# Opening of an attention and expert kernel: one more product in three float32r terms, one batch written out, another order

## The chip, the cores and the metric

The kernel runs on one core of one Trainium2 chip. The metric is the device time of one execution in microseconds (us). The kernel before takes 484.51 us, the median of three executions (484.27 to 484.58).

The core has TensorE (PE, matrix products into PSUM), VectorE (DVE), ScalarE (ACT), GpSimd (POOL, idle here), SyncE (SP, which only issues transfers here) and DMA engines that move data between HBM and SBUF.

## The reference

Inputs: `x` (8 batches, 8 heads, 512 rows, 64 columns) and `state` (8, 8, 32, 64) in float32, four weights `w1`, `w2` (512 x 1024), `w3` (1024 x 1024) and `w_out` (1024 x 512), which arrive as float64.

```python
scores = scale * x @ state.T;  a = softmax(scores);   xread = a @ state
scores2 = scale * state @ x.T; a2 = softmax(scores2); sread = a2 @ x
tokens = concat([xread, sread], axis=2)   # 544 rows a batch, 512 columns
out = ((tokens @ w1) * (tokens @ w2)) @ w3 @ w_out
```

## The kernel before, in words

The products `w3 @ w_out` are formed once (called B here, 1024 x 512), so that each batch needs only `g = (tokens w1) * (tokens w2)` and `g B`. Since `xread = a @ state`, `tokens w1` is formed as `a (state w1)`: a small product of states and weights per batch (steps `u`, line 206) and a large one with the attention weights `a` (steps `a0` to `a7`, line 440). From batch 1 on, `g B` is done in quarters with seven products (steps `P1` to `P7`); batch 0 uses plain products (steps `e` and `z`, line 584). The rows of `sread` of all batches are multiplied at the end (line 870).

**Two kinds of matrix product.** A product on float32 operands is one instruction of the program, which the trace shows as two records. For float32r operands a value is split into a high part (a cast on ScalarE, step names that end in `h`) and a low part (a subtraction on VectorE, names that end in `l`), and the product is three instructions: high by low, high by high, low by high.

**The opening.** Every weight arrives as 64-bit words and is turned into float32 in steps of one row block of 128 rows and 1024 columns (`conversion_steps`, line 674): `l` loads 1 MB (SP), `p` reads the high words (ScalarE), `u` the low words (ScalarE, a few on VectorE), `s` shifts (VectorE), `a` and `b` add (VectorE). Blocks `c0` to `c7` hold a row block of `w_out` and half of a column block of `w3`; `w4` to `w7` hold the other halves of `w3`; `q0` to `q7` hold `w1` and `w2`. B is the sum over k of products of row block k of `w3` (transposed) and row block k of `w_out`: step `f{k}` (line 749, matmuls in line 763) adds the term k for the first four row blocks of B, step `m{i}{k}` (line 786, matmuls in line 798) the term k for row block i from 4 to 7. For the k in `THIN` (line 39) `f{k}` uses three float32r terms; its operands are split by the steps `v{k}oh`, `v{k}ol` (rows of `w_out`) and `v{k}wh`, `v{k}wl` (columns of `w3`). For the k in `THIN_W3` (line 40) `m{i}{k}` does so, with the steps `V{i}h`, `V{i}l`. The steps `k...` split B.

**Attention steps of batch b.** `x` loads states and x (lines 270, 272), `sP` multiplies them (line 206), `sM` to `sl` are the two softmaxes, `sQ` a rearrangement by 16 transfers, `rP` the product for `sread`, `t` the load of x in another layout.

**What sets the order.** The order is written out by hand: `OPENING` (line 42) is a list of step names, of which `follow` (line 912) calls one after the other, and each engine gets its instructions in that order. `OPENING` covers the weights and batch 0, with pieces of batch 1. For the batches 1 to 7 `follow` runs a script (`SCRIPTS`, line 61), in which `+` stands for a step of the next batch; `CLOSING` ends the kernel. Each engine works its own list in order and waits only where a step needs the result of another engine. Transfers are all issued in one list by SP; a load into a buffer waits until the steps that read what was there before are done, and the loads behind it in the list wait with it. x of a batch is loaded into the buffer `x_d`, which in the opening first holds the words of `c4` (`HOMES`, line 36); the words of `c3` and `w4` lie in the buffer `x_s`.

Of the kernel before, what the change touches and what calls it, by code (L numbers as in the profile page):

```python
# [33 lines left out]
WARM = 15  # L34
CUTS = {"c0": (320, 640, NW), "c1": (640, NW)}
HOMES = {"c3": "x_s", "c4": "x_d", "w4": "x_s", "q0": "x_s"}
LOADS = {}
ON_DVE = ("c0u0", "c0u1", "c1u0", "c2u0")
THIN = (2, 4, 6)
THIN_W3 = {4: (2, 4, 6), 5: (2, 4, 6), 6: (2, 4, 6), 7: (2, 4, 6)}  # L40

OPENING = """
c0l c0u0 c0p0 c1l c0p1 c0p2 c0u2 c0s0 c0u1 c0s1 c1p1 c0s2 c0a0 c0b1 c0a1 c0b2 c1p0 c1u0 c1u1 c1s1 c2l c1s0 f0
c3l c4l c1b1 c2p0 c1a0 c1b0 c2u0 c5l c2s0 c2a0 f1 c2b0 v2oh v2wh c3p0 c3u0 v2ol v2wl c3s0 c4p0 c3b0 c3a0 c4s0 f2
c6l c4u0 c5p0 c4a0 v4oh f3 c7l c4b0 v4wh c5u0 v4ol v4wl c5s0 c5a0 w4l c5b0 c6p0 c6u0 w5l c6s0 c7p0 f4 c6a0 v6oh
c6b0 v6wh c7s0 c7u0 v6ol w4p0 w6l w4u0 v6wl c7b0 w5p0 w4s0 f5 c7a0 f6 w5u0 f7 w6p0 0:x 0:sP w4a0 w5s0 w5a0 V4h
w6s0 q1l V4l k0h k0l q0l w7l V5h m40 V5l 0:sT m42 k1h m47 m44 m45 q1p0 k1l m46 w6u0 0:sR q0p0 m50 q1s0 q1u0 m52
w6a0 m41 m43 w7p0 m51 w7u0 V6h k4h m55 0:sM m56 q0s0 kph q1a0 w7s0 m53 0:sN 0:sS m57 w7a0 k4l 0:sX q2l 0:sC kpl
q0u0 m54 q2p0 q3l 0:sD m60 m61 q0a0 k5h k5l q3p0 0:sF m67 V7h m63 q4l q2u0 V7l 0:sE m70 m73 m65 0:sG m77 q5l
q2s0 q3s0 V6l m71 0:sV q3u0 m75 m72 q3a0 m74 m64 0:sh q2a0 q4p0 q4u0 q6l 0:q00p 0:q01p 0:sl 0:q11p 0:q00h 0:q01h  # L50
0:q11h 0:sW q5p0 m62 0:q00l 1:x 0:q01l q4s0 m66 0:q11l q4a0 q5u0 k6h 0:q10p q5s0 m76 0:q10h q6u0 q6p0 k7h 0:a0
0:q10l q7l 0:sQ k6l q5a0 0:c0 q6s0 q7u0 0:m0 k7l 0:h0 q6a0 0:l0 0:a1 0:a2 0:c1 0:e0 q7p0 q7s0 0:m1 0:c2 0:u2p
q7a0 0:m2 0:u3p 0:a3 0:h1 0:u2h 0:u3h 0:h2 0:u2l 0:u3l 0:c3 0:l1 0:sA close 0:a5 0:a4 0:l2 g00 0:m3 0:h3 g01
0:l3 0:c5 g0A g0C 0:sB g0B 0:c4 0:m5 0:m4 1:sP 0:e1 g0D 0:e2 0:h4 0:a6 0:a7 0:h5 1:sT 0:l5 1:sR g11 1:sS 0:e3
0:l4 1:sM g10 1:sX 0:c6 0:t 0:c7 1:sC 0:m6 g0h 0:m7 2:x 1:sD 0:h7 0:e4 0:h6 1:sN g0l 0:l6 0:e5 0:e6 g1A 1:sE
0:l7 1:sF 0:e7 g1B 1:sA 0:rP g1D 1:u0p g1C 1:sB g1h 1:sG 0:rS 0:o0 1:u1p g1l 1:u2p g20 0:z3 1:sV 0:rV g21 1:u0h
1:sh g2A 0:o1 g2C 1:sl g2B 1:t 1:u0l 0:d0 g2D 1:sW 0:z2 g30 g2h g2l g3A 1:sQ g31 g3C g3B 0:d1 0:o3 1:u1h 0:o2
g3D 1:u2h 0:d3 0:rQ 1:u1l 1:u2l g3h g3l 0:d2
"""

SCRIPTS = {
# [48 lines left out]
def attn_bilinear_kernel(  # L110
# [11 lines left out]
    B, _, NT, H, D = x_s.shape  # L122
# [35 lines left out]
    def step(name):  # L158
        def keep(f):
            assert name not in steps, name  # L160
            steps[name] = f
            return f

        return keep
# [509 lines left out]
    def conversion_steps(name, src, place, wout=None):  # L674
# [7 lines left out]
        def _():  # L682
            c["out"] = place() if callable(place) else place
            room, tag, bufs = (att, HOMES[name], 1) if name in HOMES else (pool, "raw", 3)
            c["raw"] = room.tile([P, NW], mybir.dt.int64, name=tag, bufs=bufs)
            loads = LOADS.get(name, ())
            for start, stop in zip((0, *loads), (*loads, NW)):
# [39 lines left out]
    for k in range(FT):  # L727
        conversion_steps(f"c{k}", w34_k[k], chunks[k], w_out[k])

        if k in THIN:  # L730
            @step(f"v{k}oh")
# [18 lines left out]
        def _(k=k):  # L750
# [4 lines left out]
            for i in range(FT // 2):  # L755
                cols = slice(i * P, (i + 1) * P)
                if k in THIN:
                    hi, lo = thin[k, 0]
# [153 lines left out]
    def follow(script, b=None):  # L912
        for name in script.split():
            ahead = {"+": 1, "*": 2}.get(name[0], 0)
            if b is None or name[0] == "!":
                key = name.lstrip("!")
            elif b + ahead < B:
                key = f"{b + ahead}:{name.lstrip('+*')}"
            else:
                continue  # L920
            steps[key]()

    follow(OPENING)
    for b in range(1, B):
        follow(SCRIPTS.get(b, SCRIPTS[None]), b)
    follow(CLOSING)

# [43 lines left out]
```

## Time and profile before

| | us |
|---|---|
| median of three executions | 484.51 |
| the profiled execution | 484.38 |
| its span, from the first to the last instruction | 482.6 |
| TensorE: matmuls in flight | 476.6 |
| VectorE busy | 394.4 |
| ScalarE busy | 238.7 |

The rows of the trace are told apart by engine, source line and operation, with output and input tile; times are us from the start of the span. `PEld` is the load of weights into the array, which lies beside the matmuls. A matmul's record begins when it is let into the array and ends at a modelled time, so records overlap and the distance from start to start is the time that a matmul really takes of the engine. TensorE ran at the full clock (mean 0.999) through the profiled execution.

### The profile page before, as it was taken

The page shows a single profiled execution, that of the slowest core. Times are in us where ns is not written, and L with a number is a line of the kernel's source. Part 1 is how long each engine was busy: PE and PEld are TensorE (multiplying, and loading weights), DVE is VectorE, ACT ScalarE, POOL GpSimd, SP SyncE. Part 2 cuts the span into 40 slices and gives each one's busy share as a digit, 9 for nine tenths or more (in the row PEclk, how much of TensorE's full clock was granted, in tenths as well). Part 3 has the DMA queues.
Part 4 walks back from the last instruction along what each step waited for, and adds up shares of the span by engine and source line. Part 5 has one row for each costly group of instructions (what it writes and reads, how often), then busy time and mean ns, then how long its engine had stood idle before and what let it go on. Part 6 is the DMA issues. An engine that isn't in the chain of part 4 may idle for free.

```text
span 482.6 us, 8676 instructions
## 1 busy us (share of the span) xinstructions
PE 476.6 (99%) x3414; PEld 375.1 (78%) x3414; DVE 394.4 (82%) x589; ACT 238.7 (49%) x376; POOL 0.2 (0%) x4
## 2 busy tenths in 40 slices
PE   8999999999999999999999999999999999999996
PEld 6545476867779777978797879787978797899885
DVE  5899997997998599859985998599859985578870
ACT  4989784534555055505551554156425632353640
POOL 0000000000000000000000000000000000000000
PEclk9999999999999999999999999999999999999999
DMA  8999653234015304230523042304220222001001
GB/s 342 428 422 372 264 140 96 87 111 107 11 53 176 89 4 182 48 87 4 182 46 88 4 183 48 84 5 183 50 84 4 90 53 80 6 2 64 26 1 44
DMA packets 56361, 52.49 MB, mean 109 GB/s; under 512 B 42752, under 2 KB 50944, under 8 KB 51712
## 3 DMA queue, kind: packets, MB, share of 16 engines
q1 hardware_dynamic: 47488, 43.27, 26.7%
q10 hardware_dynamic: 8832, 8.65, 5.2%
q8 instruction: 27, 0.44, 0.4%
q14 instruction: 14, 0.11, 0.1%
HBM read 38.27 MB, written 8.91 MB: 98 GB/s over the span
## 4 chain that ended last, share of the span: by engine, by line
PE 97%; DMA 1%; ACT 0%; DVE 0%; issue 0%
PE ps L440 37%; PE ps_o L226 11%; PE ps L237 8%; PE ps L206 8%; PE ps_o L584 7%; PE ps_o L231 6%; PE ps_o L798 5%; PE ps L242 4%; PE ps L870 3%; PE ps_o L763 3%; PE ps L763 3%; PE ps L872 2%; PE ps_o L385 1%; DMA raw<-in_w_k_dram 1%; ACT w_sb L696 0%; PE ps L385 0%
## 5 line engine op out<-in xcount | busy, mean ns | idle before, releaser
L440 PE MATMUL ps<-at_lo,sw_hi 128*128 128x512 f32 x256 | 100.6, 393 | 0.0
L440 PE MATMUL ps<-at_hi,sw_lo 128*128 128x512 f32 x256 | 99.9, 390 | 0.0
L440 PE MATMUL ps<-at_hi,sw_hi 128*128 128x512 f32 x256 | 99.9, 390 | 0.0
L450 ACT COPY tmp<-ps 128x512 f32<-128x512 f32 x64 | 37.5, 586 | 125.0 <-PE ps L440 122.6
L440 PEld LDWEIGHTS ps<-at_lo,sw_hi 128*128 128x128 f32 x256 | 48.1, 188 | 11.1 <-issue 0.8
L440 PEld LDWEIGHTS ps<-at_hi,sw_lo 128*128 128x128 f32 x256 | 48.1, 188 | 10.1
L440 PEld LDWEIGHTS ps<-at_hi,sw_hi 128*128 128x128 f32 x256 | 48.1, 188 | 9.7
L182 DVE TENSOR_TENSOR tmp<-tmp,ps 128x512 f32<-128x512 f32 x50 | 34.3, 686 | 18.8 <-PE ps L242 17.0
L179 DVE TENSOR_TENSOR sw_lo<-ps,sw_hi 128x1024 fp32r<-128x1024 f32 (+1 forms) x34 | 38.4, 1149 | 5.4 <-ACT sw_hi L185 5.4
L465 DVE TENSOR_TENSOR g_x<-tmp,ps 128x512 f32<-128x512 f32 x28 | 19.0, 677 | 28.0 <-ACT tmp L450 28.0
L185 ACT CAST g_hi<-raw 128x512 fp32r<-128x512 f32 x42 | 24.7, 619 | 31.3 <-DVE raw L465 21.9
L185 ACT CAST sw_hi<-ps 128x1024 fp32r<-128x1024 f32 (+1 forms) x34 | 31.3, 971 | 4.5 <-PE ps L206 4.5
L226 PEld LDWEIGHTS ps_o<-t,g_hi 128*128 128x128 f32 x224 | 27.7, 190 | 5.0 <-PE ps L206 5.0
L206 PE MATMUL ps<-w_sb,st 64*32 64x512 f32 (+1 forms) x544 | 31.4, 570 | 0.0
L185 ACT CAST g_hi<-g_x 128x512 fp32r<-128x512 f32 x42 | 25.5, 626 | 11.2 <-DVE g_x L465 6.0
L179 DVE TENSOR_TENSOR g_lo<-raw,g_hi 128x512 fp32r<-128x512 f32 x42 | 27.4, 679 | 3.6 <-ACT g_hi L185 2.0
L226 PE MATMUL ps_o<-t,g_hi 128*128 128x256 f32 x224 | 29.6, 285 | 0.0
L226 PE MATMUL ps_o<-wo,g_hi 128*128 128x256 f32 x224 | 29.0, 282 | 0.0
L226 PEld LDWEIGHTS ps_o<-wo,g_hi 128*128 128x128 f32 x224 | 28.2, 189 | 0.5
L237 PE MATMUL ps<-t,g_hi 128*128 128x512 f32 x112 | 28.0, 392 | 0.0
L179 DVE TENSOR_TENSOR g_lo<-g_x,g_hi 128x512 fp32r<-128x512 f32 x42 | 27.1, 682 | 1.0 <-PE ps_o L231 1.0
L237 PEld LDWEIGHTS ps<-t,g_hi 128*128 128x128 f32 x112 | 20.2, 189 | 3.6
(139 smaller groups left out, 813.0 us busy)
## 6 DMA issues: line engine op xcount, KB each, us to landing
x_d<-in_x_d_dram SPq DMA_DIRECT2D x8, 1024.0 KB, 8.1
x_s<-in_x_s_dram SPq DMA_DIRECT2D x8, 1024.0 KB, 5.2
raw<-in_w_dram SPq DMA_DIRECT2D x7, 1024.0 KB, 7.0
out_dram<-tmp ACTq DMA_DIRECT2D x56, 128.0 KB, 1.8
raw<-in_w_k_dram SPq DMA_DIRECT2D x6, 1024.0 KB, 9.6
e<-work SPq DMA_DIRECT2D x112, 32.0 KB, 2.0
raw<-in_w3t_dram SPq DMA_DIRECT2D x3, 1024.0 KB, 6.3
sread<-turned SPq DMA_DIRECT2D x128, 4.0 KB, 1.7
```

The costliest lines, as they stand in the source:

```text
L179: nc.vector.tensor_tensor(out=out, in0=x, in1=y, op=ALU.subtract)
L182: nc.vector.tensor_tensor(out=out, in0=x, in1=y, op=ALU.add)
L185: nc.scalar.copy(out=hi, in_=src)
L206: nc.tensor.matmul(ps[j * NS:(j + 1) * NS, q], states[rows, j], moving(rows, j), start=True, stop=True)
L226: nc.tensor.matmul(ps[:, tt * HO:(tt + 1) * HO], g, w(part, k), start=(fresh and k == 0 and tt == 0 and part == "lo"), stop=False, skip_gr ...
L231: nc.tensor.matmul(ps[:, tt * HO:(tt + 1) * HO], g, w("hi", k), start=False, stop=(k == QF - 1), skip_group_check=True)
L237: nc.tensor.matmul(ps[:, tt].rearrange("p (n d) -> p n d", n=2), g, w(k), start=(k == 0), stop=False, skip_group_check=True,)
L440: nc.tensor.matmul(ps[:, i], w[:, kt, c:c + P], a[:, kt], start=(k == 0), stop=(k == 3 * KT - 1))
L450: nc.scalar.copy(out=copies[ft], in_=sums[ft][:, 0])
L584: nc.tensor.matmul(ps[:, :DO], g, wo[w][:, ft, :], start=(ft == 0 and k == 0), stop=(ft == FT - 1 and k == 2))
L763: nc.tensor.matmul(w34_ps[i][:, :DO], a, w, start=(k == 0 and n == 0), stop=(k == FT - 1 and n == len(terms) - 1))
L798: nc.tensor.matmul(w34_ps[i][:, :DO], a, w, start=(len(started) == 1 and n == 0), stop=(len(started) == FT and n == len(terms) - 1),)
```

## The change

Three things change. Row 7 joins `THIN`, so f7 is done in three float32r terms, and the steps v7oh, v7ol, v7wh and v7wl come in. Batch 1 leaves the loop: the loop starts at `LOOPED = 2`, and all steps of batch 1 (and those of batches 2 and 3 that its script held) are written into `OPENING`. The order in `OPENING` is another one throughout. `THIN_W3` is as before, so the steps m47, m57, m67 and m77 stay in float32.

```diff
+LOOPED = 2
 ON_DVE = ("c0u0", "c0u1", "c1u0", "c2u0")
-THIN = (2, 4, 6)
+THIN = (2, 4, 6, 7)
 THIN_W3 = {4: (2, 4, 6), 5: (2, 4, 6), 6: (2, 4, 6), 7: (2, 4, 6)}
 
 OPENING = """
-c0l c0u0 c0p0 c1l c0p1 c0p2 c0u2 c0s0 c0u1 c0s1 c1p1 c0s2 c0a0 c0b1 c0a1 c0b2 c1p0 c1u0 c1u1 c1s1 c2l c1s0 f0
...
+c0l c0p0 c0u0 c1l c0p1 c0u1 c0s1 c0s0 c0a1 c0a0 c0p2 c0u2 c0s2 c0b1 c1p0 c2l c3l c0b2 c1u0 c1p1 c1u1 c1s0 c1s1
...
     follow(OPENING)
-    for b in range(1, B):
+    for b in range(LOOPED, B):
         follow(SCRIPTS.get(b, SCRIPTS[None]), b)
     follow(CLOSING)
```

The line numbers of the changed kernel are higher by 7 (line 763 is 770, line 798 is 805).

VectorE at the very start, before: c0 is converted in pieces of 320, 320 and 384 columns; 128x320 rows with `ulps` are the low words (c0u0, c0u1), those on `w_sb` the shifts (c0s0, c0s1; 384 columns: c0s2), and `ISA` rows the sums, whose sizes count half words (640: c0a0, 256: c0b1, 384: c0a1, 768: c0b2).

```order
L707 TENSOR_SCALAR ulps<-raw 128x320
L714 TENSOR_SCALAR w_sb<-w_sb 128x320
L707 TENSOR_SCALAR ulps<-raw 128x320
L714 TENSOR_SCALAR w_sb<-w_sb 128x320
L714 TENSOR_SCALAR w_sb<-w_sb 128x384
L721 ISA w_sb<-w_sb,ulps 128x640
L721 ISA w_sb<-w_sb,ulps 128x256
L721 ISA w_sb<-w_sb,ulps 128x384
L721 ISA w_sb<-w_sb,ulps 128x768
```

The same place now:

```order
L714 TENSOR_SCALAR ulps<-raw 128x320
L714 TENSOR_SCALAR ulps<-raw 128x320
L721 TENSOR_SCALAR w_sb<-w_sb 128x320
L721 TENSOR_SCALAR w_sb<-w_sb 128x320
L728 ISA w_sb<-w_sb,ulps 128x384
L728 ISA w_sb<-w_sb,ulps 128x640
L721 TENSOR_SCALAR w_sb<-w_sb 128x384
L728 ISA w_sb<-w_sb,ulps 128x256
L728 ISA w_sb<-w_sb,ulps 128x768
```

The low words come first, and the short shift c0s2 has moved from before the three sums that f0 needs to before the last of them.

TensorE at the end of the f products, before: rows with `w_sb` alone on the right are float32 (f7 at the first two), those with `g_hi,tmp` and `g_lo,tmp` float32r (the row ahead is the last of f6), `x_d,st` is 0:sP, and line 798 is m40 and m42.

```order
L763 MATMUL ps_123<-g_hi,tmp 128x512
L763 MATMUL ps_o<-w_sb 128x512 x2
L763 MATMUL ps_123<-w_sb 128x512 x2
L206 MATMUL ps_277<-x_d,st 32x512 x8
L798 MATMUL ps_o<-w_sb,w_202 128x512
L798 MATMUL ps_o<-g_hi,g_x 128x512
```

Now, from f5 to the beginning of f6:

```order
L770 MATMUL ps_o<-w_sb 128x512 x2
L770 MATMUL ps_128<-w_sb 128x512 x2
L213 MATMUL ps_239<-x_d,st 32x512 x8
L770 MATMUL ps_o<-g_hi,tmp 128x512
L770 MATMUL ps_o<-g_lo,tmp 128x512
L770 MATMUL ps_o<-g_hi,tmp 128x512 x2
```

The product 0:sP has moved from behind f7 to between f5 and f6, and f7, which follows f6, is made of the same rows as f6.

SP's list of loads, before: `raw`, `x_s` and `x_d` are the buffers, `w_k` the blocks c, `w3t` the blocks w, `w` alone the blocks q, `in_st` and `in_x_d` are step 0:x.

```order
L688 DMA raw<-in_w_k_dram 128x1024 x3
L688 DMA x_s<-in_w3t_dram 128x1024
L688 DMA raw<-in_w3t_dram 128x1024 x2
L270 DMA st<-in_st_dram 128x128
L272 DMA x_d<-in_x_d_dram 128x2048
L688 DMA raw<-in_w_dram 128x1024
```

Now:

```order
L695 DMA raw<-in_w_k_dram 128x1024 x3
L277 DMA st<-in_st_dram 128x128
L279 DMA x_d<-in_x_d_dram 128x2048
L695 DMA x_s<-in_w3t_dram 128x1024
L695 DMA raw<-in_w3t_dram 128x1024 x2
L695 DMA raw<-in_w_dram 128x1024
```

The states and x of batch 0 have moved ahead of w4, w5 and w6 in the list.

## Rows read from the trace of the kernel before

**Rows 1.** The page's first part: busy us of each engine, share of the span, instructions.

```profile
PE 476.6 (99%) x3414; PEld 375.1 (78%) x3414; DVE 394.4 (82%) x589; ACT 238.7 (49%) x376; POOL 0.2 (0%) x4
```

**Rows 2.** Busy time of each engine in three stretches: start and end, length, then per engine busy us (instructions), the granted clock of TensorE, the busy share of the DMA engines, GB/s.

```profile
8.33:34.15 25.82, 25.72 (x77) 14.25 (x78) 23.80 (x39) 23.46 (x29) 0.00 (x0) 1.00 1.01 426
34.15:63.40 29.25, 29.25 (x157) 15.66 (x158) 28.30 (x36) 23.88 (x31) 0.00 (x0) 1.00 0.84 330
63.40:139.80 76.40, 76.40 (x546) 57.69 (x546) 68.63 (x107) 38.54 (x60) 0.00 (x0) 1.00 0.27 73
```

**Rows 3.** The chain of work that ended last, in order of time: start, length, engine, tile and line.

```profile
8.33 1.98 PE ps_o L763 x4
...
27.84 1.38 PE ps_o L763 x6
...
30.61 1.72 PE ps_o L763 x4
32.33 1.72 PE ps L763 x4
34.15 1.09 PE ps L206 x16
35.24 23.61 PE ps_o L798 x67
...
63.40 8.17 PE ps L440 x36
...
170.94 16.55 PE ps L440 x72
...
478.70 0.58 ACT tmp L906
```

**Rows 4.** What TensorE's matmuls waited for in the whole execution: us in total, times, longest.

```profile
PE ps_o L149 <- DVE work L146: 1.0, 1, 1.0
PE ps_o L763 <- DVE w_sb L721: 0.9, 1, 0.9
```

**Rows 5.** The end of f7 and 0:sP in order of time (start, length, engine; in brackets the idle time before), and the instruction that loads x of batch 0 (duration in ns, first and last start in us) with its time from issue to landing.

```profile
32.17 1.88 PE L763 MATMUL ps<-w_sb 128*128 128x512 f32 x4
34.15 1.09 PE L206 MATMUL ps<-x_d,st 64*32 64x512 f32 x16
...
34.12 0.21 PEld L206 LDWEIGHTS ps<-x_d,st 64*32 64x32 f32 x16 [0.90 <-issue]
...
L272 SPq DMA_DIRECT2D x_d<-in_x_d_dram x1: 423/423/423, 24.7 to 24.7; - x1
...
DMA to landing us min/median/max: 9.3/9.3/9.3
```

**Rows 6.** The issues of the loads of c4 (`x_d`) and w4 (`x_s`) in order of time, and from the page's sixth part their KB and us from issue to landing.

```profile
2.83 0.45 SPq L688 DMA_DIRECT2D x_d<-in_w_k_dram  x1
...
16.57 0.33 SPq L688 DMA_DIRECT2D x_s<-in_w3t_dram  x1
...
x_d<-in_w_k_dram SPq DMA_DIRECT2D x1, 1024.0 KB, 12.7
x_s<-in_w3t_dram SPq DMA_DIRECT2D x1, 1024.0 KB, 8.7
```

**Rows 7.** ScalarE in order of time: the starts of c0, c1 and c2 (in brackets the idle time before, and what ended it), the low words of c4, a cast of v6 and the low words of c7, then the two steps of w4.

```profile
5.69 1.32 ACT L696 ACTIVATE w_sb<-raw 128x320 f32<-128x320 f32 x3 [3.69 <-DMA raw<-in_w_k_dram]
...
8.10 1.25 ACT L696 ACTIVATE w_sb<-raw 128x384 f32<-128x384 f32 x2 [0.63 <-DMA raw<-in_w_k_dram]
...
10.54 1.18 ACT L696 ACTIVATE w_sb<-raw 128x1024 f32<-128x1024 f32 x1 [0.74 <-DMA raw<-in_w_k_dram]
...
17.43 1.19 ACT L709 ACTIVATE ulps<-x_d 128x1024 int32<-128x1024 uint32 x1
...
25.60 0.62 ACT L185 CAST tmp<-w_sb 128x512 fp32r<-128x512 f32 x1
26.13 1.16 ACT L709 ACTIVATE ulps<-raw 128x1024 int32<-128x1024 uint32 x1
27.17 1.14 ACT L696 ACTIVATE w<-x_s 128x1024 f32<-128x1024 f32 x1
28.21 1.16 ACT L709 ACTIVATE ulps<-x_s 128x1024 int32<-128x1024 uint32 x1
```

**Rows 8.** VectorE in order of time: the start of c0, the sum that completes w4, two long and two short instructions of the stretch after it.

```profile
6.70 0.71 DVE L714 TENSOR_SCALAR w_sb<-w_sb 128x320 int32<-128x320 int32 x2
7.32 1.43 DVE L721 CUSTOM_DVE_ANT_0 w_sb<-w_sb,ulps 128x640 uint16<-128x640 uint16 x4
...
29.56 1.22 DVE L721 CUSTOM_DVE_ANT_0 w<-w,ulps 128x2048 uint16<-128x2048 uint16 x1
...
43.47 1.22 DVE L179 TENSOR_TENSOR work<-work,m 128x1024 f32<-128x1024 f32 x1
44.61 1.22 DVE L721 CUSTOM_DVE_ANT_0 sw_lo<-sw_lo,ulps 128x2048 uint16<-128x2048 uint16 x1
45.74 0.68 DVE L179 TENSOR_TENSOR wo<-ps_o,wo 128x512 fp32r<-128x512 f32 x1
46.35 1.22 DVE L336 TENSOR_REDUCE sum<-work 128x32 f32<-128x1024 f32 x1
```

**Rows 9.** ScalarE's longest wait for a load between 25 and 62 us: us in total, times, longest.

```profile
ACT w_sb L696 <- DMA raw<-in_w_dram: 2.2, 1, 2.2
```

More of the change, by code (lines that the diff above doesn't have):

```diff
@@ L36 @@
 HOMES = {"c3": "x_s", "c4": "x_d", "w4": "x_s", "q0": "x_s"}
+LOOPED = 2
 LOADS = {}
 ON_DVE = ("c0u0", "c0u1", "c1u0", "c2u0")
-THIN = (2, 4, 6)
+THIN = (2, 4, 6, 7)
 THIN_W3 = {4: (2, 4, 6), 5: (2, 4, 6), 6: (2, 4, 6), 7: (2, 4, 6)}
 OPENING = """
-c0l c0u0 c0p0 c1l c0p1 c0p2 c0u2 c0s0 c0u1 c0s1 c1p1 c0s2 c0a0 c0b1 c0a1 c0b2 c1p0 c1u0 c1u1 c1s1 c2l c1s0 f0
-c3l c4l c1b1 c2p0 c1a0 c1b0 c2u0 c5l c2s0 c2a0 f1 c2b0 v2oh v2wh c3p0 c3u0 v2ol v2wl c3s0 c4p0 c3b0 c3a0 c4s0 f2
-c6l c4u0 c5p0 c4a0 v4oh f3 c7l c4b0 v4wh c5u0 v4ol v4wl c5s0 c5a0 w4l c5b0 c6p0 c6u0 w5l c6s0 c7p0 f4 c6a0 v6oh
@@ L46 @@
[L46 to L55, printed above, removed]
@@ L56 @@
-0:l7 1:sF 0:e7 g1B 1:sA 0:rP g1D 1:u0p g1C 1:sB g1h 1:sG 0:rS 0:o0 1:u1p g1l 1:u2p g20 0:z3 1:sV 0:rV g21 1:u0h
-1:sh g2A 0:o1 g2C 1:sl g2B 1:t 1:u0l 0:d0 g2D 1:sW 0:z2 g30 g2h g2l g3A 1:sQ g31 g3C g3B 0:d1 0:o3 1:u1h 0:o2
-g3D 1:u2h 0:d3 0:rQ 1:u1l 1:u2l g3h g3l 0:d2
+c0l c0p0 c0u0 c1l c0p1 c0u1 c0s1 c0s0 c0a1 c0a0 c0p2 c0u2 c0s2 c0b1 c1p0 c2l c3l c0b2 c1u0 c1p1 c1u1 c1s0 c1s1
+c1b0 c1a0 c1b1 f0 c2p0 c4l c5l c2u0 c2s0 c2b0 c2a0 v2wh v2oh c3p0 v2wl v2ol c3s0 c3u0 c6l c3b0 c4p0 c3a0 c4u0
+c4s0 c4b0 f1 c7l c5p0 c4a0 v4wh v4wl f2 v4oh v4ol c5s0 c5u0 c6p0 f3 0:x c6u0 c5a0 c5b0 f4 c6s0 c7p0 c6a0 c7u0
@@ new lines @@
+c6b0 c7s0 v6wh f5 w4l 0:sP w5l v6oh c7a0 c7b0 v7oh w4p0 v7wh w6l v6ol v6wl w4u0 w5p0 v7ol f6 w4s0 v7wl 0:sT f7
+k0h q1l q0l w4a0 k0l 0:sR w5s0 w5u0 V4h w6p0 m40 V4l k1h m45 0:sS w7l m43 w5a0 m44 q1p0 m47 m42 k1l 0:sM 0:sX
+m50 w6s0 q1s0 q1u0 m46 w6u0 m41 V5h m55 w7p0 0:sC k4h m57 V5l q1a0 m52 q0p0 w7u0 w6a0 m51 k4l q2l m54 m56 V6h
+m53 0:sD m60 q0s0 q2p0 m63 kph 0:q01p m67 k5h 0:sF V6l 1:x 0:sN w7s0 0:sG w7a0 m66 k5l 0:sE q3l m70 0:sV q0u0
+q0a0 q5l q2s0 q3p0 m71 m77 q2u0 m73 m65 V7h q3u0 V7l m74 m76 kpl q3s0 m61 q2a0 0:q01h 0:sh q3a0 q5p0 m64 0:q00p
@@ new lines @@
+0:q01l 0:q11p q5u0 q7l 0:q10p 0:q00h 0:sl 0:q11h m62 q4l q7p0 0:q00l q7u0 m75 k6h 0:a0 q5s0 m72 0:q10h q6l
+0:q11l q4p0 0:a1 q5a0 0:c0 k6l q7s0 0:q10l 0:a2 0:m0 q7a0 q4s0 q6p0 0:h0 k7h 0:l0 q6u0 q4u0 q6s0 0:c1 0:c2 k7l
+q6a0 0:e0 q4a0 0:m1 0:m2 0:u3p 0:sW 0:h1 0:u3h 0:u2p 0:u2h 0:u3l close 0:a3 0:u2l 0:l1 0:sA 0:c3 g01 0:a4 0:a5
+0:m3 0:h3 0:l3 0:c4 0:m4 0:h2 0:l2 g00 g0A 0:a7 0:h4 g0B 0:c5 0:sQ g0C 0:m5 0:t 1:sP 0:l4 g0D 0:c7 1:sT 0:a6
+0:m7 0:h7 g10 0:e1 0:e2 1:sM 0:c6 g0h 1:sR 0:m6 0:h5 1:sN 0:h6 0:e3 0:l5 0:sB 0:e4 0:e5 0:l6 0:e6 0:l7 1:sE 1:sS
@@ new lines @@
+1:sX g0l 1:sC 0:e7 g11 0:rP g21 1:t g1A 0:rS 1:sD g1B g1C 1:u1p 0:o0 g1D 1:sF 1:u1h 0:o1 1:u0p 1:sG 0:d1 1:sV
+g1h g20 1:u0h 1:sA g1l 1:u2p 0:z2 g2A g2C 1:sW 2:x 1:u2h 1:sh 0:rV g2B 1:sB g2D 1:u0l 1:u1l 1:sl 0:z3 0:d0 0:o3
+0:d3 1:a0 1:a1 1:u2l 1:c0 0:o2 1:sQ 1:m0 1:u3p g2h 1:c1 1:u3h 2:sP 1:rP g30 g2l 0:d2 1:m1 g31 1:u3l 2:sM 1:a2
+1:c2 2:sN 2:sT g3A g3B 2:sR 2:sS 1:a3 2:sE 1:m2 1:c3 1:a4 0:rQ g3C 2:sX 1:m3 1:A0h g3D 1:rS g3h 1:B1d 2:sC 1:a6
+g3l 1:A1h 1:a5 1:B1h 2:sD 1:A0l 2:sF 1:c6 2:sA 3:x 1:c4 1:c5 1:m4 1:B1l 1:m6 1:a7 1:B0d 2:sG 2:sV 1:A1l 1:B0h
@@ L59 @@
+1:m5 1:c7 1:m7 1:rV 1:B0l 2:sW 1:C0h 1:D0x 1:P1 1:P2 1:E0h 2:u0p 1:E0l 1:D1x 2:u2p 1:v2 1:C1h 2:sQ 2:u1p 1:C0l
+1:v1 1:C1l 2:u0h 1:D0y 1:P3 1:D1y 1:E1h 1:E1l 1:P4 1:G0h 1:rQ 2:u0l 2:u2h 1:F0h 1:F1h 1:v3 1:F1l 1:D0z 1:H0h
+2:u2l 1:G1h 2:t 1:G1l 2:u1h 1:F0l 1:d3 1:P5 2:u1l 1:D1z 1:v5a 1:G0l 1:H0l 1:H1h 2:sh 1:v5b 1:H1l 1:v5c 2:sl 1:P6
+1:v6a 1:v6b 2:sB 1:v6c 1:P7 1:v7a 1:v7b 1:d5 1:d6 1:d7
 """
```

## Prediction

> **What bounds the kernel now.** I read the summary of the engines first [rows 1]: TensorE has a matmul in flight for 99% of the span, VectorE 82%, ScalarE 49%. A share of busy time alone would not settle it, so I went to TensorE's waits: the whole execution has two, of 1.0 and 0.9 us, both before the first real matmul at 8.33 us [rows 4]. Then the chain of work that ended last [rows 3]: from 8.33 us it is TensorE alone, piece against piece, until the closing copy at 478.70 us, and its pieces run at their own pace: 72 float32r matmuls of 512 columns in 16.55 us are 230 ns each, in the middle of the loop as well as in the opening. The table of stretches [rows 2] says the same for the part that is rewritten: TensorE is busy for all but 0.1 us of 8.33 to 139.80 us, while VectorE has 28.3 of 29.25 us between 34.15 and 63.40 us and is nearly full too.
>
> So a new order can win time in three ways only: less work on TensorE, an earlier first matmul, or the closing of the one small hole that a busy share hides. All else that moves on VectorE and ScalarE is worth nothing while TensorE has its operands in time, and costs as soon as it has not.
>
> **The hole.** The step 0:sP (line 206, states against x of batch 0) starts at 34.15 us. The four records before it begin at 32.17 [rows 5]; such records stand 430 ns apart (four in 1.72) [rows 3], so the array was free at 33.89: 0.26 us unused. The weight load of 0:sP came at 34.12 after 0.90 us, and the transfer of x, issued at 24.70, landed 9.3 us later, at 34.0 [rows 5]. This is a wait for x.
>
> **The change, part by part, against the profiled execution (484.38 us, 0.13 below the median of 484.51).**
>
> *f7 in three terms.* f6, already in three float32r terms, takes 2.77 us on the chain (27.84 to 30.61); f7, four plain float32 matmuls of two records each, takes 3.44 (30.61 to 32.33, then 1.72) [rows 3]. With f7 like f6, TensorE has 0.67 us less, which is what I take. By the Trainium skill, "FP8 and Floating Point Precision", section "TensorE Precision Notes", a true float32 product is four passes through the array; three passes in their place would save a quarter of 3.44, or 0.86 us, and the sum below would end at 483.6. The trace agrees only in part: a float32r pass takes 230 ns here, more than a quarter of a float32 product's 860 [rows 3].
>
> *What it adds.* Two casts on ScalarE (v7oh, v7wh; a cast of 512 columns starts at 25.60 and the next step at 26.13, so 0.53 each) [rows 7] and two subtractions on VectorE (v7ol, v7wl; 0.61 from the start at 45.74 to the next at 46.35) [rows 8]: 1.1 and 1.2 us. They lie beside TensorE's f5 and f6. VectorE has 0.95 us idle from 34.15 to 63.40 and some 7.8 us from 63.40 to 139.80 [rows 2], so they cost nothing in the end unless a matmul has to wait for the operands behind them; that is the question of the next steps.
>
> *0:sP two products earlier.* It now stands between f5 and f6, some 6 us earlier in TensorE's row, and the transfer of x is issued before w4, w5 and w6. Landings come 2.4 to 2.45 us apart (ScalarE starts on c0, c1 and c2 at 5.69, 8.10 and 10.54) [rows 7]. c4, issued at 2.83, landed after 12.7 us at 15.5; w4, issued at 16.57, after 8.7 at 25.3 [rows 6]; between them lie c5, c6, c7, so c7 lands at 22.8. x goes into the place of c4, free when the step that ends at 18.6 (17.43 + 1.19) [rows 7] is done, so it is queued in time to follow c7. Alone it would take 2.45 us like the others; before, it came 3.8 us behind w6 (34.0, against 25.3 + 2 x 2.45 = 30.2). It lands between 25.3 and 26.6. f5 ends at 27.8. So 0:sP doesn't wait: the 0.26 us go.
>
> *The price of it.* w4 lands at 27.8 to 29.1 instead of 25.3. ScalarE began on w4 at 27.17 [rows 7]; with one more cast ahead it can at 27.7. So w4's two steps with v7wh between them end between 30.5 and 31.8 (1.04 + 0.53 + 1.16), and VectorE, which now does w4s0, v7wl, 0:sT and w4a0 in this order (two short and two long, 0.60 + 0.61 + 1.13 + 1.22, from the end of w4p0 at 28.9 to 30.2), has w4 ready at 32.5 to 33.8. TensorE reaches m40 at 34.3 (27.8 + 1.0 + 2 x 2.75). Before, w4 was ready at 30.78 (29.56 + 1.22) [rows 8] for an m40 at 35.2 [rows 3]: 4.4 us of cover shrink to 0.5 to 1.8. Nothing is lost, but little is left.
>
> *The first product of batch 0 (0:a0).* It starts at 63.40 [rows 3]. Now TensorE gets there at 61.8: 0.67 and 0.26 earlier, and 0.69 because m72 (three matmuls of 230 ns) stands behind 0:a0. On VectorE the order puts between w4a0 and 0:q00l, the last split that 0:a0 needs, 15 long instructions at 1.13 us from start to start (43.47 to 44.61), 13 short ones at 0.60 (45.74 to 46.35) [rows 8], and seven smaller ones, which I put at 2.4 us together: 27.2 us, so 0:q00l ends at 59.7 to 61.0 if VectorE never waits. It waited 0.95 us in this stretch before [rows 2]. With that the cover is -0.2 to 1.2 us; I book 0.15 us for it.
>
> *The first matmul.* The two shifts and the low-word scalings of c0 are in a new order, but the short shift c0s2 still stands ahead of the last sum (now c0b1, before c0a1) that f0 needs. c0s1 must wait for ScalarE's second piece, about 6.6 us (two of the three pieces that take 1.32 from 5.69) [rows 7]; from there two shifts, two sums, one shift and one sum of the lengths in [rows 8] end at about 8.35. f0 starts 0 to 0.1 us later; I book 0.05.
>
> *Batch 1 written out.* TensorE has there the same instructions, and no hole to close: 16.55 us for 72 in the chain. VectorE's steps are spread otherwise; 0:sW and the g steps go later. I book nothing, with 0 to 0.3 us at risk where a split stands just ahead of its product. The joints on TensorE between float32 and float32r are a few more in the w3 products (20 blocks against 16); bounds -0.1 to +0.2 us, I take 0.05.
>
> Sum: -0.67 - 0.26 + 0.15 + 0.05 + 0.05 = -0.68 on 484.38 gives 483.70; with the 0.13 of the median, **483.8 us**. A measurement of this kernel can tell about 0.2%, or 0.97 us, from no change: all that the change can win, 0.93 us, is just under that.
>
> **The rivals.** *Part of it is given back* (B). VectorE and ScalarE reach 0:a0, or m50 or m70, late by up to 1.5 us. For it: the cover that fell from 4.4 to 0.5 us. Against: ScalarE's one long wait for a load, 2.2 us for q1 [rows 9], need not come again, since q1 lands when it did and ScalarE comes to it later. Time 483.9 to 485.4, the middle 484.4.
>
> *Slower* (C). One mechanism: x ahead of w4 makes the two helpers the bound up to 0:a0. If x takes its 3.8 us and ScalarE keeps its 2.2 us behind it, VectorE its 0.95, then 0:q00l ends at 61.0 + 2.2 + 0.95 = 64.2 and 0:a0 starts 2.4 us late: 483.65 (the sum without the 0.15) + 2.4 = 486.1. It decides from 1.8 us of lateness on. Against it: the later loads follow each other at 2.4 us, and the waits of before came where ScalarE was ahead of them, which now it is not.
>
> *More than the sum* (D). By the Trainium skill, "Perfetto Trace Analysis", section "Identifying the Most-Contended Engine", a matmul's busy share doesn't show how near TensorE is to its peak; the busy share of the weight loads does. Here that is 78% [rows 1], which would leave room. By the rows, loads lie beside matmuls that follow each other at 230 ns without a hole [rows 3], so the room isn't in the order. If the new order let only one in a hundred of the 130 us to 139.80 be packed closer, 1.3 us more would go: 482.5.
>
> *That the change doesn't do what it says* I exclude for f7 and 0:sP: the order shows both.
>
> **Chances.** The forecast (483.4 to 484.1) 0.66; B 0.22; C 0.09; D 0.03. The forecast's lower edge touches the bound of 483.54, for which I give 0.16 of its 0.66, with D 0.19 for faster; C and the upper edge of B give 0.10 for slower, and 0.71 is left for no change. The range 483.4 to 485.0 leaves out C, D and the top of B.
>
> **What would show it.** Right: TensorE's waits stay at two; f7 takes 2.75 us; 0:sP follows f5 with no weight load waiting; the first L440 matmul near 61.8 us; every later piece earlier by the same 0.7 us. Wrong: a wait of TensorE for VectorE at the w3 products (now line 805) or at 0:a0, with ScalarE's casts or loads behind VectorE; or ScalarE waiting for w4 until after 29 us. A start of f0 before 8.2 us would make it faster than I say.

## The result, and the profile after

The changed kernel takes **487.98 us** in the median of 6 executions (487.04 to 488.61), the kernel before 484.51: a ratio of 1.0071, interval 1.0059 to 1.0084. It is 3.5 us slower; I had said 483.8 and 483.4 to 485.0. The profiled execution took 488.61 us.

The page's first part answers to [rows 1]; the shares look as before:

```profile
PE 477.9 (98%) x3418; PEld 376.1 (77%) x3418; DVE 396.0 (81%) x591; ACT 241.2 (50%) x378; POOL 0.2 (0%) x4
```

TensorE's waits, which were two [rows 4], are three (line, what ended the wait, us in total, times, longest):

```profile
PE ps_o L392 <- DMA out_dram<-tmp: 2.3, 1, 2.3
PE ps_o L770 <- DVE w_sb L728: 1.7, 1, 1.7
PE ps_o L156 <- DVE work L153: 1.0, 1, 1.0
```

The first is new; the other two lie ahead of f0, as before. Line 392 is the step 2:rP: 64 small matmuls that read batch 2's tokens `x_s` (the x of batch 2 in the other layout, which step 2:t loads) with its probabilities. The chain of work that ended last (start, length, what), which in [rows 3] was TensorE alone from 8.33 us on, now leaves it for SyncE's queue (SPq). Pieces of it, from the opening to 2:rP:

```profile
27.88 1.02 PE ps L213 x16
28.90 1.59 PE ps_o L770 x6
30.49 1.36 PE ps L770 x6
31.85 1.36 PE ps_o L770 x6
33.21 1.36 PE ps L770 x6
34.57 14.82 PE ps_o L805 x42
...
62.49 2.76 PE ps L447 x12
...
155.91 1.84 SPq L220
...
164.13 1.72 DMA sread<-turned
...
166.33 5.74 DMA out_dram<-tmp
172.07 2.40 PE ps_o L392 x64
```

Up to 62 us nearly all is as I had it: 0:sP (L213) follows f5 at once, f7 (the last two L770 pieces) takes 2.72 us, w3's products begin at 34.57 (forecast 34.3) and 0:a0 at 62.49 (forecast 61.8). The trouble is 100 us later. SyncE's queue (start, length of the group, line, transfers) says why; first the changed kernel:

```profile
120.33 10.77 SPq L220 DMA_DIRECT2D sread<-turned  x16
131.21 0.52 SPq L277 DMA_DIRECT2D st<-in_st_dram  x1
131.83 0.38 SPq L279 DMA_DIRECT2D x_d<-in_x_d_dram  x1
144.08 10.49 SPq L220 DMA_DIRECT2D e<-work  x16
154.62 11.37 SPq L220 DMA_DIRECT2D sread<-turned  x16
166.03 0.65 SPq L284 DMA_DIRECT2D x_s<-in_x_s_dram  x1
```

and the kernel before:

```profile
120.42 21.03 SPq L213 DMA_DIRECT2D sread<-turned  x32
141.55 0.53 SPq L277 DMA_DIRECT2D x_s<-in_x_s_dram  x1
142.12 0.43 SPq L270 DMA_DIRECT2D st<-in_st_dram  x1
142.59 0.43 SPq L272 DMA_DIRECT2D x_d<-in_x_d_dram  x1
150.69 10.81 SPq L213 DMA_DIRECT2D e<-work  x16
```

The load of batch 2's tokens (2:t) was issued at 141.55 us, ahead of 2:sQ (`e<-work`). In batch 1 written out it stands behind 2:sQ, which waits for 2:sW until 144.08, and behind 1:rQ (`sread<-turned`). SyncE gives out one of these small transfers in 0.65 to 0.7 us, 16 in 10.5 to 11.4, so the tokens are issued at 166.03 us, and they land 5.9 us later, at 171.9. TensorE is through with 3:sP (16 matmuls from 168.68 us, about 1.0 us) at 169.7 and stands until 172.06. The rows of 3:sP, of 2:rP and of the first product of 2:a2 in the kernel before:

```profile
168.84 1.06 PE L206 MATMUL ps<-x_d,st 64*32 64x512 f32 x16
169.84 1.10 PE L385 MATMUL ps_o<-x_s,e 128*32 128x64 f32 x64
170.87 0.50 PE L440 MATMUL ps<-at_lo,sw_hi 128*128 128x512 f32 x1
```

and now (in brackets the idle time before):

```profile
168.68 1.06 PE L213 MATMUL ps<-x_d,st 64*32 64x512 f32 x16
172.06 2.41 PE L392 MATMUL ps_o<-x_s,e 128*32 128x64 f32 x64 [2.32 <-DMA out_dram<-tmp]
174.40 0.80 PE L447 MATMUL ps<-at_lo,sw_hi 128*128 128x512 f32 x1
```

Then comes what no row of before had shown: TensorE's clock. By stretches (start and end, length, busy us and instructions of each engine, granted clock, DMA share, GB/s):

```profile
168.00:172.00 4.00, 1.75 (x32) 0.31 (x16) 3.41 (x6) 2.54 (x4) 0.00 (x0) 1.00 0.64 262
172.00:174.00 2.00, 1.94 (x62) 1.83 (x63) 1.77 (x3) 0.00 (x0) 0.00 (x0) 0.63 0.03 8
174.00:176.00 2.00, 2.00 (x18) 1.54 (x11) 1.49 (x4) 0.00 (x0) 0.00 (x0) 0.52 0.00 0
176.00:178.00 2.00, 2.00 (x11) 1.60 (x10) 0.23 (x2) 0.00 (x0) 0.00 (x0) 1.00 0.02 2
```

From 172.5 to 175.9 us TensorE runs at the lower of its two levels, 1.2 GHz instead of 2.4 (cut finer, the granted clock is 1.00 up to 172.5 us, 0.50 from 172.75 to 175.75 and 1.00 again from 176.0). Starts of the same step, after minus before, give the account: 3:sP -0.16 us, 2:rP +2.22, 2:a2 +3.53, what follows 2:a7 +4.27. So 2.38 us are the standstill; 1.31 and 0.74 are 2:rP and the first products of 2:a2, slower than before. The 4.27 us are what the profiled execution lost (488.61 against 484.38).

The label of the wait, `out_dram<-tmp` (a store of results, issued by ScalarE's queue and not by SyncE's), is not its cause: the tokens land at the same moment, at 171.9 us. In a second profiled execution of the same kernel (486.71 us, in the group `after_again` below) the same row names the load itself:

```profile
PE ps_o L392 <- DMA x_s<-in_x_s_dram: 2.6, 1, 2.6
```

Its rows around the standstill (start, length, in brackets the idle time before):

```profile
168.09 1.06 PE L213 MATMUL ps<-x_d,st 64*32 64x512 f32 x16
171.76 1.54 PE L392 MATMUL ps_o<-x_s,e 128*32 128x64 f32 x64 [2.60 <-DMA x_s<-in_x_s_dram]
173.22 0.50 PE L447 MATMUL ps<-at_lo,sw_hi 128*128 128x512 f32 x1
```

Here the clock stays at 2.4 GHz. 3:sP is 0.75 us earlier than before, 2:rP 1.92 later, 2:a2 2.35 later: 2.67 us of standstill, and 0.43 more because 2:rP's matmuls take 1.46 us from the first to 2:a2, not 1.03.

### The profile page after: what moved, and what is told of

Its sections match the earlier page's. It is cut to its first block, busy times and chain, and to the rows that moved or that the text cites. A ratio compares the mean times of both kernels' runs of the same rounds, so it can differ in the third digit from the quotient of the medians.

```text
span 486.8 us, 8682 instructions
## 1 busy us (share of the span) xinstructions
PE 477.9 (98%) x3418; PEld 376.1 (77%) x3418; DVE 396.0 (81%) x591; ACT 241.2 (50%) x378; POOL 0.2 (0%) x4
## 4 chain that ended last, share of the span: by engine, by line
PE 90%; SPq 4%; DMA 3%; DVE 2%; issue 1%; ACT 1%; ACTq 0%; DVEq 0%
PE ps L447 34%; PE ps_o L233 10%; PE ps_o L591 7%; PE ps L244 7%; PE ps L213 7%; PE ps_o L805 5%; PE ps_o L238 5%; SPq L220 4%; PE ps L249 4%; PE ps L877 3%; PE ps_o L770 3%; PE ps L770 3%; PE ps_o L392 2%; PE ps L879 2%; DMA out_dram<-tmp 1%; DMA raw<-in_w_k_dram 1%
## 5 line engine op out<-in xcount | busy, mean ns | idle before, releaser
L189 DVE TENSOR_TENSOR tmp<-tmp,ps 128x512 f32<-128x512 f32 x50 | 34.3, 686 | 16.0 <-PE ps L249 14.2
L213 PE MATMUL ps<-w_sb,st 64*32 64x512 f32 (+1 forms) x544 | 31.7, 571 | 0.0
```

The source lines that it names most:

```text
L189: nc.vector.tensor_tensor(out=out, in0=x, in1=y, op=ALU.add)
L213: nc.tensor.matmul(ps[j * NS:(j + 1) * NS, q], states[rows, j], moving(rows, j), start=True, stop=True)
```

## The experiments

**The tokens first.** In the changed kernel's order, one word moved:

```diff
-1:c6 2:sA 3:x 1:c4 ... 1:G1h 2:t 1:G1l
+1:c6 2:sA 2:t 3:x 1:c4 ... 1:G1h 1:G1l
```

> The changed kernel with one word of the order moved: the load of batch 2's tokens (2:t) stands ahead of 3:x, behind 0:rQ, so SyncE issues it at some 131 us, before the 16 transfers of 2:sQ and the 16 of 1:rQ. Main theory (TensorE waits at 2:rP for these tokens, and its clock falls because of this wait): 2:rP starts at 169.83 - 0.16 = 169.7 us without a wait, no stretch at 1.2 GHz behind it, 2:a7 and all after it 0.16 us earlier than in the kernel before; 484.51 - 0.16 = 484.35 us. Rival 1 (the wait is for batch 2's states, 2:sQ, or for the sorted rows of 1:rQ, whose transfers don't move): 2:rP still starts near 172 us and the time stays at 488. Rival 2 (the wait is for the tokens, but the clock falls for another reason): 2:rP on time, the slow stretch stays, 484.35 + 2.0 = 486.4 us.

Measured: 483.69 us (ratio 0.9982, interval 0.9973 to 0.9991), no wait at 2:rP, granted clock 0.999 or 1.0 in all 11 executions. The chain is TensorE's again:

```profile
167.37 1.88 PE ps L212 x32
169.25 1.03 PE ps_o L391 x64
170.28 16.55 PE ps L446 x72
```

One place on SyncE's list is the whole loss. The expectation was 0.66 us too high: I had taken the changed kernel's -0.16 us ahead of 2:rP from its one profiled execution. Here 0:a1 is 0.70 us earlier than before, and 2:rP (169.18) and the end of the chain 0.66. The profiled execution of the changed kernel had given 0.5 us back between m40 and 0:a0 that this one did not.

**The tokens late, their use later.** SyncE's list stays, TensorE gets other work first (batch 2 gets a script of its own):

```diff
-+sP +sM rP rS +sN +sT rV rQ +t *x
-a2 c2 m2 +sE +sR +sA +sS
++sP +sM +sN +sT
+a2 c2 m2 rP rS rV rQ +t *x +sE +sR +sA +sS
```

> The changed kernel with the order of SyncE left as it is (the tokens of batch 2 issued at 166 us), and the step that needs them, 2:rP, moved behind 2:a2, 2:c2 and 2:m2 in batch 2's own script. Main theory: TensorE has 2:a2 (some 2 us) and what follows it to do while the tokens land at 172.1 us, so the wait falls from 2.3 us to under 0.5, the clock stays at 2.4 GHz, and the time is 484.4 to 484.9 us. Rival 1 (something else than the use of the tokens stops TensorE at 169.8 us, as the states or an operand of 2:a2): the wait stays at 2.3 us, now ahead of 2:a2, and the time at 488. Rival 2 (clock falls for another reason): 486.4 us.

Measured: 483.88 us (0.9987, interval 0.9978 to 0.9996), below the expectation for the same reason. The tokens are issued at 165.52 us, as late as in the changed kernel:

```profile
165.52 0.76 SPq L302 DMA_DIRECT2D x_s<-in_x_s_dram  x1
```

2:a2 starts at 169.13 and 2:rP at 172.07, and TensorE's only two waits, of 1.0 us each, lie ahead of f0:

```profile
169.13 0.50 PE L465 MATMUL ps<-at_lo,sw_hi 128*128 128x512 f32 x1
...
172.07 1.10 PE L410 MATMUL ps_o<-x_s,e 128*32 128x64 f32 x64
```

Late tokens cost only where something stops for them; 0.2 us remain against the tokens first.

**Between the two.** 2:t behind 2:sQ, ahead of 1:rQ:

```diff
-1:G0h 1:rQ 2:u0l ... 1:G1h 2:t 1:G1l
+1:G0h 2:t 1:rQ 2:u0l ... 1:G1h 1:G1l
```

> The changed kernel with the tokens of batch 2 behind 2:sQ and ahead of 1:rQ: issued at 154.7 us, landed near 160.7. Theory (only the moment counts at which they land, against 169.2 us when TensorE comes to 2:rP; 2:sQ alone ahead of them is harmless): no wait, no fall of the clock, 483.7 us as with the tokens ahead of both. Rival (the order of 2:sQ and the tokens matters by itself, by the buffer or the DMA engines): between 484.5 and 488.

Measured: 483.61 us (0.9982, interval 0.9973 to 0.9991). The tokens are issued at 154.16 us, with 10.5 us of 2:sQ ahead of them, and nothing waits. So 16 transfers ahead of the tokens cost nothing and 32 do; the next two kernels have 30 and 36.

**Two doses.** 1:rQ split, 14 transfers ahead of 2:t and 2 behind; and 1:rQ whole with its first 4 transfers issued once more ahead of 2:t (written short: in brackets, which of the 16 transfers are issued there).

```diff
-1:rQ ... 2:t
+1:rQ[0:14] 2:t 1:rQ[14:16]
```

```diff
-1:rQ ... 2:t
+1:rQ[0:16] 1:rQ[0:4] 2:t
```

> The changed kernel with 14 of the 16 transfers of 1:rQ ahead of the tokens of batch 2 and 2 behind them. Each takes SyncE some 0.65 us, so the tokens are issued about 1.4 us earlier (164.6 us) and land near 170.7. Main theory (2:rP waits for the tokens, and what comes on top is TensorE's clock): the wait is 1.0 to 1.5 us. If the fall of the clock needs the long wait, the time is 483.69 + 1.2 = 484.9 us and no stretch at 1.2 GHz is seen; if any wait here brings it, 483.69 + 1.2 + 2.0 = 486.9 us. Rival (the tokens' load is held by something else than its turn on SyncE): 488 as before.

> The changed kernel with the first 4 transfers of 1:rQ issued a second time behind 1:rQ (the same data to the same place), ahead of the tokens of batch 2, so that these are issued some 2.6 us later, at 168.6 us, and land near 174.7. Main theory: TensorE's wait ahead of 2:rP grows one for one from 2.3 - 2.9 us to 5 - 5.5; with the loss at 1.2 GHz as it was (2.0 us), 487.98 + 2.6 = 490.6 us. If the loss grows with the wait, more: 491 to 493. Rival (SyncE's list isn't the bound): 488.

Measured: 485.75 us (1.0037, interval 1.0019 to 1.0055) and 489.49 (1.0105, interval 1.0091 to 1.0118). With 14, the 10 executions lie apart: 484.59 to 485.85 us at a granted clock of 0.998 to 1.0 over the whole run, 487.71 to 488.05 at 0.996. Neither of my two cases: the lower clock comes in some executions only. The profiled one had issued the tokens at 163.59 us, stood for 0.4 and kept its clock; how long the four slower ones stood is not shown. With 20, the tokens leave at 167.84 and the wait, to which the view gives no transfer, is

```profile
PE ps_o L393 <- issue: 3.1, 1, 3.1
```

instead of 5: the tokens left 0.8 us earlier than I had put it, the load needed 5.2 us, not 6, and 3:sP ended 0.2 us later. All four executions were at 0.996 to 0.997. More transfers ahead, a later 2:rP: that holds (169.51, 172.06 and 173.02 us with 14, 16 and 20 of the second group ahead); the slope I had expected was too steep.

**The standstill filled.** The changed kernel with 3:sP's matmuls run three times over (the same products into the same place), beside the changed kernel itself on the same chip.

```diff
-            per_head(s["ps"], s["st"], lambda rows, j: s["x"][rows, j])
+            for _ in range(3 if b == 3 else 1):
+                per_head(s["ps"], s["st"], lambda rows, j: s["x"][rows, j])
```

> The changed kernel with the same late tokens, and the 16 matmuls of 3:sP (the states against x of batch 3, the last work ahead of 2:rP) run three times over, the same products into the same place: TensorE has some 2.0 us more to do while the tokens come in. In the executions so far the time falls in two groups by the granted clock of the whole run: with 14 of 16 transfers ahead 484.6 to 485.9 at 0.998 - 1.0, 487.7 to 488.1 at 0.996. Theory (the standstill of 2.3 to 2.9 us brings the stretch at 1.2 GHz, the late tokens alone cost only the wait): 2:rP still starts near 172 us, the wait shrinks to under 1 us, no stretch at 1.2 GHz: 483.7 + 2.3 to 2.9 = 486.0 to 486.6 us at 1.0. Rival (the stretch at 1.2 GHz belongs to the late start or to the matmuls of 2:rP themselves, not to the standstill): 488 at 0.996.

> The changed kernel as it is, beside the one before on the same chip, for the spread of its executions: 487.0 to 488.6 us, most of them at a granted clock of 0.996.

Measured: 486.69 us (1.0047, interval 1.0034 to 1.0060) filled, 487.37 (1.0060, interval 1.0046 to 1.0073) as it is. Filled, the wait was

```profile
PE ps_o L393 <- DMA out_dram<-tmp: 0.7, 1, 0.7
```

and 2:rP started at 171.75, as late as ever. One execution in five was at 0.996 (487.82 us), the others at 485.90 to 486.73. As it is, three were at 0.996 (488.03 to 488.32) and three at 1.0 (485.98 to 486.71), so with the first six, 8 of 12. That points to the standstill as what lets the clock fall, but five executions don't settle it, and one fell with the standstill filled.

**f7 by itself.** The kernel before with f7 in three terms; to serve it, the two casts, the two subtractions and a few helper steps beside them stand ahead of f5:

```diff
-THIN = (2, 4, 6)
+THIN = (2, 4, 6, 7)
-c7s0 c7u0 v6ol w4p0 w6l w4u0 v6wl c7b0 w5p0 w4s0 f5 c7a0 f6 w5u0 f7
+c7s0 c7u0 v6ol w4p0 w6l v6wl c7a0 c7b0 v7oh v7wh w4u0 w4s0 v7ol v7wl w5p0 f5 f6 w5u0 f7
```

> The kernel before with f7 in three float32r terms and nothing else (its two casts and two subtractions put ahead of f5). f7 alone is worth 3.44 - 2.77 = 0.67 us of TensorE's work. Theory: here 0:sP still stands behind f7 and the tokens of batch 0 still land at 34.0 us, so the 0.67 us turn into a wait for them: TensorE gets to 0:sP at 33.2 us and starts it at 34.1; nothing is won, 484.4 to 484.5 us. Rival (the transfer isn't the bound, it comes earlier or the hole of before was something else): 484.51 - 0.67 = 483.84 us.

Measured: 484.60 us (1.0001, interval 0.9992 to 1.0010): nothing won. f7 is shorter, and the time becomes a longer wait for x, where [rows 5] had a short one:

```profile
34.42 1.09 PE L206 MATMUL ps<-x_d,st 64*32 64x512 f32 x16 [1.20 <-DMA x_d<-in_x_d_dram]
```

**The other way out, and its mend.** The same, with 0:sP behind m40, where x has long landed; then also k0h and k0l, the split of the first finished block, moved ahead.

```diff
-... w4a0 w5s0 0:sP w5a0 ... m40 V5l 0:sT
+... w4a0 w5s0 w5a0 ... m40 V5l 0:sP 0:sT
```

```diff
-f7 w6p0 0:x w4a0 w5s0 w5a0 V4h w6s0 q1l V4l k0h k0l
+f7 k0h w6p0 0:x w4a0 w5s0 k0l w5a0 V4h w6s0 q1l V4l
```

> The kernel before with f7 in three float32r terms and 0:sP moved the other way, behind m40, so that it meets tokens that have landed long before. Theory (the two sums that I took for TensorE hold, and the rest of the order of before has cover for both): f7 -0.67 us, the hole ahead of 0:sP -0.26 us: 484.51 - 0.93 = 483.6 us. Rival (the helpers have no cover: VectorE, full from 34 to 63 us, is late at m50 or at 0:a0, as it was in the changed kernel, which gave 0.55 of 0.75 us back): 484.0 to 484.2 us.

> The kernel of e6_f7_and_sP_late (f7 in three terms, 0:sP behind m40 in the order of before; 485.96 us, 2.2 us of wait at m40) with k0h and k0l, the split of the first finished block, put ahead of w6p0 and w5a0. Theory (m40 waits for VectorE's k0l, which ends at 35.4 us there and frees the PSUM bank, not for w4, complete at 31.6 us): k0h 1.4 us and k0l some 1.5 us earlier, m40 at 33.4 to 33.9 us instead of 35.45, and 1.5 to 2.0 us less in all if nothing else is late behind it: 484.0 to 484.5 us. Rival (the helpers as a whole are late, so that the wait moves to m42 or m50): 485 to 486 us.

Measured: 485.96 us (1.0041, interval 1.0028 to 1.0054) and 484.48 (1.0000, interval 0.9991 to 1.0009). In the first, m40 waits 2.2 us for VectorE:

```profile
30.41 1.22 DVE L721 CUSTOM_DVE_ANT_0 w<-w,ulps 128x2048 uint16<-128x2048 uint16 x1
...
34.71 0.68 DVE L179 TENSOR_TENSOR wo<-ps_o,wo 128x512 fp32r<-128x512 f32 x1
...
35.45 1.12 PE L798 MATMUL ps_o<-w_sb,w 128*128 128x512 f32 x2 [2.20 <-DVE wo L179]
```

The row at 34.71 is k0l, the split of the block that f7 finishes first. w4 was complete at 31.6 us already (30.41 + 1.22). With k0l earlier m40 starts at

```profile
33.77 1.12 PE L798 MATMUL ps_o<-w_sb,w 128*128 128x512 f32 x2 [0.48 <-DVE wo L179]
```

and 1.48 us come back, nearly the 1.5 to 2.0 expected, but no gain over before remains: at m47 TensorE is 0.18 us ahead, at 0:a0 0.14 behind. Both sums that I counted, 0.93 us, can be given back in full by helpers that an order doesn't serve in time.

**f7 plain.** The kernel with the tokens first, f7 in plain float32 again:

```diff
-THIN = (2, 4, 6, 7)
+THIN = (2, 4, 6)
```

> The kernel with the tokens first (483.69 us), with f7 in plain float32 again, without its two casts and two subtractions; x early and 0:sP behind f5 stay. If f7's 0.67 us are won in full here: 483.69 + 0.67 = 484.36 us, m40 at 35.1 us, and 0:a0 0.67 later too. Rival (the helpers, not TensorE, set the pace up to 0:a0, so that f7 is worth less): m40 at 35.1, but 0:a0 by less than 0.4 us later, 483.7 to 484.1 us.

Measured: 484.17 us (0.9994, interval 0.9985 to 1.0003), 0.48 us above the tokens first. f7's two pieces take 3.43 us on the chain (32.01 to 35.44) against 2.72, so 0.7 of TensorE's work are worth about 0.5 to 0.6 in the end: 0:a1 is 0.69 us later in the profiled execution, of which 0.10 are a later start of f0, and the medians say 0.48 (0.54 if each is set against the kernel before on its own chip, 0.82 and 0.28 us). What stays below before, 0.3 us, fits the 0.26 of the hole.

## Why the prediction was wrong, and where it was right

**The step that failed** is "Batch 1 written out: ... no hole to close ... I book nothing, with 0 to 0.3 us at risk where a split stands just ahead of its product." I went through TensorE's instructions and VectorE's splits there, and not through SyncE's list, though 0:x in the opening had just shown me what a place on it is worth. Before, 2:t stood ahead of 2:sQ; the rewritten list puts it behind 2:sQ and 1:rQ, 32 small transfers; at 0.65 to 0.7 us each from 144.08 us that is 166 us, some 6 us of landing make 172, and 2:rP was due at 169.2. The pace (16 transfers of `e<-work` in 10.81 us) and 2:rP's place right behind 3:sP could have been had from before's own rows; the 144.08 us are the changed kernel's, but before's 150.69 us for the start of 2:sQ would have shown the danger too. The cost was not 0 to 0.3 but 2.4 to 2.7 us of standstill, 0.4 us of a slower 2:rP, and about 1.5 us of clock in 8 of 12 executions (487.76 to 488.61 us against 485.98 to 487.04).

**None of the rivals was it.** C had the right direction by luck: its mechanism, helpers that make 0:a0 2.4 us late, was not there (0:a0 at 62.49 us, where C had 64.2), and what cost the time lies 100 us behind it. B is real but small: 0.5 us given back in the profiled execution, none in the second. Of the 0.5 us, 0.33 are the weight loads ahead of 0:a0 that waited for VectorE's `sw_lo`, which VectorE ended 1.2 us later than in the second execution; why it was late there stays open. In the order of before B is large: with 0:sP behind m40 all that follows came 1.5 us later than before. D didn't show; TensorE's pieces keep their 16.55 us for 72.

**What held.** Without the late tokens the kernel takes 483.69 us, in the trace 0.66 us less than before, against my sum of -0.68. That the two agree to 0.02 us is partly luck: m40 starts 0.76 us earlier than before (34.41 against 35.17), not the 0.88 of my terms (f6's first piece on the chain takes 1.59 us behind 0:sP, 1.38 behind f5 before), and behind m40 0.10 us are given back, not the 0.20 that I had booked. By terms: f7 2.72 us (forecast 2.75). 0:sP: x issued at 18.7 us, landed 6.8 later at 25.5 (forecast 25.3 to 26.6), ahead of f5's end; its row stands right behind f5's last four records:

```profile
26.00 1.88 PE L770 MATMUL ps<-w_sb 128*128 128x512 f32 x4
27.81 1.09 PE L213 MATMUL ps<-x_d,st 64*32 64x512 f32 x16
28.83 0.50 PE L770 MATMUL ps_o<-g_hi,tmp 128*128 128x512 f32 x1
```

The first product of batch 0 came later than forecast (61.8): on the chain at 62.49 us in the profiled execution, 61.91 in the second, 62.01 with the tokens first. f0 within 0.05 us of before in all three. By the Trainium skill, "FP8 and Floating Point Precision", section "TensorE Precision Notes", a true float32 product is four passes through the array; the estimate from that was 0.86 us for f7, and the runs show 0.71.

**Right number, wrong reason:** the cover at m40. I reckoned when w4 would be ready (32.5 to 33.8 us; it was at 32.95, 31.77 + 1.18). But m40 also waits for k0l, the split of the first finished block, which I had not put in the row:

```profile
33.68 0.69 DVE L186 TENSOR_TENSOR wo<-ps_o,wo 128x512 fp32r<-128x512 f32 x1 [0.73 <-ACT wo L192]
```

It ends at 34.37 and m40 starts at 34.42, right when f7 is through; here it cost nothing, but the cover was 0.05 us and not 0.5 to 1.8. In the kernel before it wasn't 4.4 us either: k0l ends at 34.41 (33.73 + 0.68) there, 0.76 us ahead of m40. In the order of before with f7 shorter and 0:sP behind m40, the wait for k0l was 2.2 us.

## What to carry to other kernels

When a list of steps is rewritten, go through it once for each queue as well: for every load, add up what is issued ahead of it at the queue's own pace, add its landing, and set the sum against the moment its first reader is due. A short standstill of TensorE can cost more than its length: in 8 of 12 executions here the run's granted clock was lower too, for some 1.5 us more. And read the same kernel's time in more than one execution before a half microsecond is explained.

## What was not expected of the hardware

A granted clock of the run below 0.998 came only in kernels in which TensorE stands still in the middle of full work: in 8 of 12 executions of the changed kernel (2.3 to 2.7 us of standstill where profiled), 4 of 10 with 14 transfers ahead, 4 of 4 with 20, 2 of 5 with 2.2 us at m40 (487.4 instead of 485.9 us), 1 of 5 with the standstill filled (0.7 us left where profiled). In the two such executions that were profiled (488.61 us, and 489.52 with 20 transfers ahead) the stretch at 1.2 GHz begins within 0.5 us of the standstill's end (172.06 to 172.5 us, 173.02 to 173.1); where the others lost theirs is not shown. In the 43 executions of the four kernels without a wait in the middle, in 22 with 0.5 us at m40 or 1.2 at 0:sP, and in those of before on the same chips, it stayed at 0.998 or above. Why it falls in one execution and not in the next after the same kind of wait stays open; none of these runs tells it. Further, the same 64 matmuls took 1.46 us behind a standstill of 2.6 us (1.47 behind 0.7, 1.61 behind 0.4) and 1.03 without, all at 2.4 GHz; that was seen and not looked into.
